# A fused attention and two-MLP kernel: column sums ordered behind the weight conversions, smaller conversion pieces, and a longer lag between the MLP's two products

## The chip, the cores and the metric

The kernel runs on one core of a Trainium2 chip. The metric is the time of one execution on the device in microseconds (us), and the profile is one execution recorded by the hardware. Its engines are PE (TensorE: matmuls; PEld are its weight loads), DVE (VectorE), ACT (ScalarE), POOL (GpSimd) and SP (SyncE, which here issues the DMAs). Each engine works through its own queue in a fixed order.

## The reference, cut to what matters

```python
attn_out = _attn_ref(q, k, v)             # 4 x 8 heads, 576 positions, 64 wide; window of 128, bias by distance
x = attn_out.transpose(0, 2, 1, 3).reshape(2304, 512)
h = x @ moe_w_in                          # 512 x 2048
g = s * np.maximum(h, 0) ** 2 + b
x = g @ moe_w_out                         # 2048 x 512
h = np.maximum(x @ moe2_w_in, 0)
return h * h @ moe2_w_out
```

`s` and `b` are single numbers, so the kernel computes the first MLP without them and applies them to its result: it is scaled by `s`, and `b` times the column sums of `moe_w_out` is added. The weights reach the kernel as 64-bit floats, that is as two 32-bit words each.

## The kernel before, in words

**Blocks.** The 2304 rows of x are worked on in nine blocks of 256: eight blocks (batch 0 to 3, first and second 256 positions) and one "tail" block, with the last 64 positions of every batch. Attention of a block goes by pairs of heads (`pair_unit`): scores on PE (L245), bias and row maximum on DVE (L186), exponentials on ACT (L190), division by the row sum on DVE (L268), transposes on PE (L270), product with v on PE (L281), and a split of the result into two parts (high and low) for the MLP.

**The MLP.** `mlp` runs over 16 steps f for each block: `first` makes a 128-row piece of the hidden layer (twelve matmuls, L357), ACT and DVE square it and split it into high and low (L367, L368, L99, L102), and `last` adds its share to the output (twelve matmuls, L394 in the first MLP; L403 in the second). Between the two lies a lag: `last` of a step is placed after `first` of the step that comes LAG = 2 later, and 1 later in the second MLP, whose blocks are 512 rows wide. The squared and split piece lies in a tile `g` with three buffers (`gw`, two buffers, for the wide blocks). `behind` is a list of pieces of other work (attention units, loads, conversions) that are placed between the steps, spread over the share `span` of them. The last two blocks of the first MLP, block 7 and the tail, run as one `mlp` call, the tail's steps six behind (`lead`); their `behind` holds `sum_column` (the product of the column sums with ones, L544, and its scaling by b) and two `fetch_y` (loads of first-MLP results and half results, and scaling by s and b, for the second MLP).

**The weights.** Each MLP's weights are four groups of four steps (512 of 2048 hidden columns). `group_loads` makes for each group a list of loads and a list of conversions. A load brings a part of w_in or w_out to a staging tile `st` (L151, on SP's queue). `convert` then turns the pairs of words into a 32-bit float and splits it in high and low: ACT on the low word (L119), DVE joins the sign (L120), ACT scales the high word (L121), DVE shifts it (L122), POOL adds the two (L123), ACT copies the high part (L99), and DVE subtracts it (L102). For the first MLP a conversion handles a whole load: parts of 128x1024 (twice the width of one step's piece; 14 of these), and for the last group's w_out four of 128x512. The second MLP has 32 parts of 128x512. The staging tiles of the first three groups are the places of the fourth group's weights, so a load waits until the conversion before it in that place is done. The second MLP's weights take the places of the first one's.

**The column sums.** `sum_rows` (L499 to L502) adds the high and low parts of each of 16 row blocks of w_out to `csum`, 32 additions on POOL. In the program they stand between the steps of blocks 3 to 6.

**The order of work.** The program is written as one sequence, with `zipped` mixing lists in given ratios. A planner then orders each engine's instructions: earlier in the program means a higher priority, but what is ready by its simulated timeline may go ahead of what isn't, as the column sums do. `tc.issue_after(x)` makes the instructions that it encloses come after x on the engine of x.

## Time and profile before

| | us |
|---|---|
| median of three runs | 1007.93 (1007.28 to 1010.74) |
| profiled execution | 1010.16 |
| its span, first to last instruction | 1008.4 |
| PE busy in the span | 974.3 (97%) |
| DVE busy | 522.2 (52%) |
| ACT busy | 490.2 (49%) |
| POOL busy | 130.4 (13%) |
| mean granted PE clock | 0.985 of full speed |

The span is shown below in 40 slices of 25.2 us; each digit is the busy share in tenths (9 is 90% or more), PEclk the granted clock in tenths, and DMA the share of the 16 DMA engines. The first slices hold the attention's first units and the conversion of the first MLP's weights, slices 20 to 27 the conversion of the second MLP's.

```profile
PE   6899889999999999999999899999999999999997
DVE  6997998443564444544265787754223222432222
ACT  7977766454555445554355666664222312322221
POOL 4653655000000000000010312310000000000000
PEclk9799989999999999999999999999999999999999
DMA  8135423111221211211052444422000100100001
```

### The profile page before, as it was taken

To read this page: it belongs to the slowest core of one execution; us is meant where nothing else is said; L and a number is where in the kernel's file an instruction comes from. 1 tells how busy PE (TensorE), PEld (TensorE's weight loads), DVE (VectorE), ACT (ScalarE), POOL (GpSimd) and SP (SyncE) were. 2 spreads that over 40 slices of the span, in tenths; PEclk is the share of its full clock that TensorE was granted. 3 is DMA by queue.
4 is the path that set the end of the run, shared out by engine and by line. 5 is a ranking of instruction groups with operands and counts; after the bars stand their busy time and mean duration, and the time that the engine had idled before them with its cause. 6 is when DMAs were issued, how large, how long until landed. Compare 5 with 4: busy or idle time off the path is not lost.

```text
span 1008.4 us, 16815 instructions
## 1 busy us (share of the span) xinstructions
PE 974.3 (97%) x6504; PEld 854.1 (85%) x6504; DVE 522.2 (52%) x1236; ACT 490.2 (49%) x1157; POOL 130.4 (13%) x118
## 2 busy tenths in 40 slices
PE   6899889999999999999999899999999999999997
PEld 4689778999989999899999888778888888898886
DVE  6997998443564444544265787754223222432222
ACT  7977766454555445554355666664222312322221
POOL 4653655000000000000010312310000000000000
PEclk9799989999999999999999999999999999999999
DMA  8135423111221211211052444422000100100001
GB/s 333 43 129 167 162 88 106 53 53 35 60 67 46 72 34 52 75 54 39 9 184 74 131 173 147 147 83 74 11 1 5 59 1 0 43 1 22 1 1 42
DMA packets 46928, 72.39 MB, mean 72 GB/s; under 512 B 6656, under 2 KB 27136, under 8 KB 46848
## 3 DMA queue, kind: packets, MB, share of 16 engines
q1 hardware_dynamic: 46848, 71.32, 21.8%
q8 instruction: 51, 0.84, 0.3%
q14 instruction: 29, 0.24, 0.1%
HBM read 59.77 MB, written 11.53 MB: 71 GB/s over the span
## 4 chain that ended last, share of the span: by engine, by line
PE 75%; DVE 9%; DMA 9%; ACT 4%; issue 2%; SPq 0%; POOL 0%; ACTq 0%; DVEq 0%; POOLq 0%
PE ob L403 15%; PE hb L357 14%; PE ha L357 13%; PE oa L394 13%; DMA st<-w_in 4%; PE oc L394 3%; PE s L245 3%; PE hc L357 3%; PE u L281 3%; DMA st<-w_out 2%; PE hbtail L357 2%; PE t L270 2%; PE obtail L403 2%; DVE wol L102 1%; DVE wil L102 1%
## 5 line engine op out<-in xcount | busy, mean ns | idle before, releaser
L394 PE MATMUL oa<-ga,woh 128*128 128x256 f32 x960 | 189.6, 289 | 7.3 <-ACT ga L99 3.9
L403 PE MATMUL ob<-woh,gb 128*128 128x512 f32 x512 | 168.9, 391 | 1.4 <-ACT gb L99 1.3
L394 PEld LDWEIGHTS oa<-ga,woh 128*128 128x128 f32 x960 | 152.2, 192 | 14.0 <-DVE ga L102 5.2
L394 PE MATMUL oa<-ga,wol 128*128 128x256 f32 x480 | 135.6, 286 | 0.1
L368 DVE SCALAR_TENSOR_TENSOR rb<-hb,rb 128x512 f32<-128x512 f32 x64 | 44.1, 690 | 147.4 <-ACT rb L367 147.2
L403 PEld LDWEIGHTS ob<-woh,gb 128*128 128x128 f32 x512 | 95.9, 188 | 23.8 <-ACT gb L99 3.3
L367 ACT ACTIVATE rb<-hb 128x512 f32<-128x512 f32 x64 | 38.2, 597 | 156.5 <-PE hb L357 152.0
L123 POOL TENSOR_TENSOR st<-st 128x512 int32<-128x512 int32 (+1 forms) x50 | 70.3, 1407 | 235.1 <-DVE st L122 177.4
L403 PE MATMUL ob<-wol,gb 128*128 128x512 f32 x256 | 99.7, 389 | 0.0
L394 PEld LDWEIGHTS oa<-ga,wol 128*128 128x128 f32 x480 | 92.2, 192 | 1.2 <-issue 0.9
L368 DVE SCALAR_TENSOR_TENSOR ra<-ha,ra 128x256 f32<-128x256 f32 x120 | 50.0, 419 | 62.9 <-ACT ra L367 62.4
L102 DVE TENSOR_TENSOR ga<-ra,ga 128x256 fp32r<-128x256 f32 x120 | 65.8, 552 | 29.0 <-ACT ga L99 28.4
L99 ACT ACTIVATE ga<-ra 128x256 fp32r<-128x256 f32 x120 | 49.5, 416 | 42.4 <-DVE ra L368 41.7
L102 DVE TENSOR_TENSOR gb<-rb,gb 128x512 fp32r<-128x512 f32 x64 | 45.5, 711 | 44.0 <-ACT gb L99 43.8
L367 ACT ACTIVATE ra<-ha 128x256 f32<-128x256 f32 x120 | 45.0, 378 | 43.6 <-PE ha L357 39.0
L99 ACT ACTIVATE gb<-rb 128x512 fp32r<-128x512 f32 x64 | 40.4, 632 | 47.7 <-DVE rb L368 35.6
L120 DVE SCALAR_TENSOR_TENSOR st<-st 128x512 int32<-128x512 int32 (+1 forms) x50 | 47.3, 950 | 26.3 <-ACT st L119 25.8
L119 ACT ACTIVATE st<-st 128x512 int32<-128x512 uint32 (+1 forms) x50 | 40.5, 814 | 35.2 <-DMA st<-w_out 19.3
L403 PEld LDWEIGHTS ob<-wol,gb 128*128 128x128 f32 x256 | 48.1, 188 | 9.7
L190 ACT ACTIVATE pr<-pr,nd 128x256 f32<-128x256 f32 (+1 forms) x96 | 45.1, 473 | 3.8 <-DVE nd L186 3.4
L121 ACT ACTIVATE st<-st 128x512 f32<-128x512 f32 (+1 forms) x50 | 40.5, 813 | 7.0 <-DVE st L120 7.0
L186 DVE CUSTOM_DVE_ANT_0 pr<-s,bases 128x256 f32<-128x256 f32 (+1 forms) x96 | 32.1, 386 | 19.4 <-PE t L270 15.0
(204 smaller groups left out, 2387.1 us busy)
## 6 DMA issues: line engine op xcount, KB each, us to landing
st<-w_out SPq DMA_DIRECT2D x20, 512.0 KB, 3.9
st<-w_in SPq DMA_DIRECT2D x8, 1024.0 KB, 6.8
st<-w_in SPq DMA_DIRECT2D x16, 512.0 KB, 4.8
st<-w_out SPq DMA_DIRECT2D x6, 1024.0 KB, 8.9
raw<-qkv SPq DMA_DIRECT2D x36, 128.0 KB, 2.6
xib<-acc SPq DMA_DIRECT2D x9, 512.0 KB, 4.4
out<-obb SPq DMA_DIRECT2D x16, 256.0 KB, 2.0
raw<-qkv SPq DMA_DIRECT2D x24, 160.0 KB, 2.9
```

Source lines behind the costliest of these rows:

```text
L99: return nc.scalar.activation(o, i, AF.Copy)
L102: nc.vector.tensor_tensor(o, a, b_, ALU.subtract)
L119: nc.scalar.activation(l32, l32.bitcast(U32), AF.Copy, scale=2.0 ** -29)
L120: nc.vector.scalar_tensor_tensor(l32, h32, -2 ** 31, l32, ALU.bitwise_and, ALU.bitwise_or)
L121: nc.scalar.activation(h32.bitcast(F32), h32.bitcast(F32), AF.Copy, scale=2.0 ** -112)
L123: nc.gpsimd.tensor_tensor(l32, h32, l32, ALU.add)
L190: nc.scalar.activation(pr, pr, AF.Exp, bias=nmx, scale=-1.0, accum_out=den)
L357: nc.tensor.matmul(ph, w_[:, cc, j * P:(j + 1) * P], x_[:, cc, :], start=(k == 0), stop=(k == 3 * NCC - 1))
L367: nc.scalar.activation(r, ph, AF.Relu)
L368: nc.vector.scalar_tensor_tensor(r, ph, 0.0, r, ALU.max, ALU.mult)
L394: nc.tensor.matmul(po[o // 2][:, (o % 2) * BLK:(o % 2 + 1) * BLK], w_[:, j, o * P:(o + 1) * P], g[:, gi, :], start=(start and n == 0 and o ...
L403: nc.tensor.matmul(po[t], g[:, gi, t * P:(t + 1) * P], w_[:, j, :], start=(start and n == 0), stop=(stop and n == 2))
```

## The change

Four things change. The 32 additions of the column sums come after the last conversion's addition on POOL (`adds[-1]`; when `sum_rows` runs, all of the first MLP's conversions are in the program, and none of the second's). A load of the first MLP's weights is converted in pieces of 128x512, two for a load of twice that, and the lists that mix conversions with other work take correspondingly more of them at a time. Once the attention is done (`"bp" in pools`) the lag is 4 instead of 2 where the block is 256 wide, and two of every five steps take their `g` from the buffers of `gw`, which makes five tiles. And in the call for the last two blocks of the first MLP, two empty entries stand ahead of `sum_column`, with a span of 0.6 instead of 0.9.

```diff
@@ -104,6 +104,7 @@
 
     n_g = [0]
 
+    adds = []
     marks = []
 
     def convert(words, hi, lo):
@@ -120,7 +121,7 @@
         nc.vector.scalar_tensor_tensor(l32, h32, -2 ** 31, l32, ALU.bitwise_and, ALU.bitwise_or)
         nc.scalar.activation(h32.bitcast(F32), h32.bitcast(F32), AF.Copy, scale=2.0 ** -112)
         nc.vector.tensor_scalar(h32, h32, 3, None, ALU.logical_shift_left)
-        nc.gpsimd.tensor_tensor(l32, h32, l32, ALU.add)
+        adds.append(nc.gpsimd.tensor_tensor(l32, h32, l32, ALU.add).ins)
         split(hi, lo, l32.bitcast(F32), act_copy, dve_sub)
 
     last_load = []
@@ -150,15 +151,18 @@
             with tc.issue_after(last_load[0]) if last_load else nullcontext():
                 wdma.append(nc.sync.dma_start(t, src).ins)
 
-        def conv(i):
+        def conv(i, y):
             _, k, n, step = parts[i]
             if k not in wts[g]:
                 for j in (k, k + 1):
                     wts[g][j] = wp.tile([P, GF, DM], F32R, tag=f"{GTAGS[j]}{g}", name=f"{GTAGS[j]}{g}")
             hi, lo = wts[g][k], wts[g][k + 1]
-            part = (slice(None), slice(n, n + step)) if k else (slice(None), slice(None), slice(n * P, (n + step) * P))
-            convert(places.pop(i).rearrange("p a (n w) -> p a n w", w=2), hi[part], lo[part])
-        return [[lambda f=f, i=i: f(i) for i in range(len(parts))] for f in (load, conv)]
+            at = slice(n + y, n + y + 1) if k else slice((n + y) * P, (n + y + 1) * P)
+            part = (slice(None), at) if k else (slice(None), slice(None), at)
+            words = places[i].rearrange("p a (n w) -> p a n w", w=2)
+            convert(words[:, y:y + 1] if k else words[:, :, y * P:(y + 1) * P], hi[part], lo[part])
+        return [[lambda i=i: load(i) for i in range(len(parts))],
+                [lambda i=i, y=y: conv(i, y) for i, part in enumerate(parts) for y in range(part[3])]]
 
 
     first = {}
@@ -362,7 +366,10 @@
                 gh = pools["bp"].tile([P, 2, w], F32R, tag="gw", name=f"g{nm}_{f}")
                 r = pools["bp"].tile([P, w], F32, tag="rw", name=f"r{nm}_{f}", bufs=1)
             else:
-                gh = mp.tile([P, 2, BLK], F32R, tag="g", name=f"g{nm}_{f}", bufs=3)
+                if "bp" in pools and n_g[0] % 5 > 2:
+                    gh = pools["bp"].tile([P, 2, 2 * BLK], F32R, tag="gw", name=f"g{nm}_{f}")[:, :, :BLK]
+                else:
+                    gh = mp.tile([P, 2, BLK], F32R, tag="g", name=f"g{nm}_{f}", bufs=3)
                 r = mp.tile([P, BLK], F32, tag="r", name=f"r{nm}_{f}")
             nc.scalar.activation(r, ph, AF.Relu)
             nc.vector.scalar_tensor_tensor(r, ph, 0.0, r, ALU.max, ALU.mult)
@@ -381,7 +388,7 @@
                 behind.pop(0)()
             first(f, n)
             done += 1
-            if len(todo) > (1 if w > BLK else LAG):
+            if len(todo) > (1 if w > BLK else 4 if "bp" in pools else LAG):
                 last()
         while todo:
             last()
@@ -479,17 +486,17 @@
     new_x(blocks[0])
     a0 = [lambda hp=hp: first_pair(0, hp) for hp in range(H // 2)]
     run(a0[:2] + l0[:1])
-    run(zipped((a0[2:], 1), (c0, 1), (l0[1:], 1)))
+    run(zipped((a0[2:], 1), (c0, 2), (l0[1:], 1)))
     new_x(blocks[1])
     a1 = [lambda hp=hp: first_pair(1, hp) for hp in range(H // 2)]
     xs = [xt[blocks[0]], xt[blocks[1]]]
-    half(0, zipped((l1, 1), (c1, 1), (a1, 2)))
+    half(0, zipped((l1, 1), (c1, 2), (a1, 2)))
     a2 = attn(2)
     half(1, zipped((a2, 3), (l2, 1)))
     xs.append(xt[blocks[2]])
     a3 = attn(3)
-    half(2, zipped((c2, 2), (a3[:2], 1)))
-    other(0, zipped((l3, 2), (c3, 2), (a3[2:5], 1)), 0.6)
+    half(2, zipped((c2, 4), (a3[:2], 1)))
+    other(0, zipped((l3, 2), (c3, 3), (a3[2:5], 1)), 0.6)
     pending = a3[5:] + attn(4)
     for i in range(1, NHALF):
         other(i, pending[:4])
@@ -498,8 +505,9 @@
     nc.sync.dma_start(b_sb, b_in.partition_broadcast(P))
     def sum_rows(g, j):
 
-        for w in (wts1[g][2], wts1[g][3]):
-            nc.gpsimd.tensor_tensor(csum, csum, w[:, j, :].bitcast(F32), ALU.add)
+        with tc.issue_after(adds[-1]):
+            for w in (wts1[g][2], wts1[g][3]):
+                nc.gpsimd.tensor_tensor(csum, csum, w[:, j, :].bitcast(F32), ALU.add)
 
     nc.gpsimd.memset(csum, 0.0)
     sums = [lambda g=g, j=j: sum_rows(g, j) for g in range(NG) for j in range(GF)]
@@ -556,7 +564,7 @@
     y0 = []
     mlp([(f"a{i}", xt.pop(blocks[i]), finish1(f"a{i}", acc_dram[i])),
          (f"a{LAST}", x_tail, finish1(f"a{LAST}", acc_dram[LAST]))], wts1, second_t, FS,
-        [sum_column] + [lambda u=u: y0.append(fetch_y(u)) for u in range(2)], 0.9, 6)
+        [lambda: None] * 2 + [sum_column] + [lambda u=u: y0.append(fetch_y(u)) for u in range(2)], 0.6, 6)
 
     def in_bp(i, nm):
         return bp.tile([P, 1, 2 * DM], I32, tag="st", name=nm, bufs=3)
```

## Rows read from the trace of the kernel before

**Rows 1.** The page, part 1: busy time, its share, instructions of each engine.

```profile
PE 974.3 (97%) x6504; PEld 854.1 (85%) x6504; DVE 522.2 (52%) x1236; ACT 490.2 (49%) x1157; POOL 130.4 (13%) x118
```

**Rows 2.** Engine time by stretch: us, busy us (instructions), granted clock, DMA share, GB/s.

```profile
10.00:50.00 40.00, 34.57 (x160) 23.57 (x161) 37.81 (x88) 39.02 (x95) 17.61 (x11) 0.82 0.43 162
50.00:110.00 60.00, 59.70 (x503) 53.40 (x503) 52.36 (x115) 43.25 (x99) 27.66 (x17) 0.98 0.47 159
110.00:140.00 30.00, 22.95 (x156) 18.54 (x155) 29.11 (x45) 20.93 (x47) 19.50 (x12) 0.83 0.38 123
140.00:160.00 20.00, 20.00 (x166) 19.52 (x164) 16.00 (x23) 11.79 (x22) 11.55 (x8) 1.00 0.25 81
170.00:210.00 40.00, 40.00 (x352) 37.14 (x350) 18.71 (x64) 20.15 (x54) 0.00 (x0) 1.00 0.12 37
560.00:600.00 40.00, 34.59 (x259) 32.04 (x258) 30.21 (x53) 26.80 (x58) 8.55 (x8) 1.00 0.46 152
680.00:1000.00 320.00, 320.00 (x1502) 268.62 (x1501) 96.98 (x151) 84.38 (x153) 0.00 (x0) 1.00 0.05 17
```

**Rows 3.** Timeline of VectorE, 128 to 136 us: start, us, line, operation, count.

```profile
128.77 4.17 DVE L268 TENSOR_SCALAR pr<-pr,nd 128x256 f32<-128x256 f32 x4
132.86 1.21 DVE L120 SCALAR_TENSOR_TENSOR st<-st 128x1024 int32<-128x1024 int32 x1
134.66 0.67 DVE L120 SCALAR_TENSOR_TENSOR st<-st 128x512 int32<-128x512 int32 x1
```

**Rows 4.** VectorE by line and form, 168 to 210 us: busy us, mean ns of one.

```profile
L102 DVE TENSOR_TENSOR gc<-rc,gc 128x256 fp32r<-128x256 f32 x13 | 6.4, 489 | 4.0 <-ACT gc L99 4.0
L268 DVE TENSOR_SCALAR pr<-pr,nd 128x256 f32<-128x256 f32 x12 | 3.4, 346 | 0.0
```

**Rows 5.** GpSimd by line and form, 110 to 140 us.

```profile
L123 POOL TENSOR_TENSOR st<-st 128x1024 int32<-128x1024 int32 x3 | 7.6, 2538 | 8.9 <-DVE st L122 8.9
L502 POOL TENSOR_TENSOR csum<-csum,woh 128x512 f32<-128x512 f32 x4 | 6.6, 1652 | 3.3 <-ACT woh L99 3.0
L502 POOL TENSOR_TENSOR csum<-csum,wol 128x512 f32<-128x512 f32 x4 | 5.3, 1325 | 0.2
L123 POOL TENSOR_TENSOR st<-st 128x512 int32<-128x512 int32 x1 | 1.0, 1044 | 1.9 <-DVE st L122 1.9
```

**Rows 6.** Timeline of TensorE, 46 to 133 us; in brackets idle time before, and its releaser.

```profile
48.70 0.38 PE L357 MATMUL ha<-x0h,wih 128*128 128x256 f32 x1 [2.41 <-DVE ra L368]
...
130.13 0.41 PE L270 MATMUL t<-ident,pr 128*128 128x128 f32 x2 [1.65 <-DVE pr L268]
131.38 0.69 PE L270 MATMUL t<-ident,pr 128*128 128x128 f32 x2 [0.85 <-DVE pr L268]
132.82 0.47 PE L270 MATMUL t<-ident,pr 128*128 128x128 f32 x1 [0.75 <-ACT pt L99]
```

**Rows 7.** The tile csum: duration ns (least, median, most), first and last start.

```profile
L502 POOL TENSOR_TENSOR csum<-csum,woh x16: 1271/1456/2250, 38.0 to 165.4; 128x512 f32<-128x512 f32 x16
L502 POOL TENSOR_TENSOR csum<-csum,wol x16: 1263/1352/2340, 41.5 to 167.1; 128x512 f32<-128x512 f32 x16
L544 PE MATMUL pc<-ones,csum x8: 250/250/271, 503.7 to 504.5; 128*128 128x1 f32 x8
```

**Rows 8.** The chain that ended last, 488 to 590 us: start, us, what.

```profile
488.56 1.44 PE ha L357 x12
584.46 5.47 DMA xib<-acc
```
**Rows 9.** ScalarE by line and form, whole span.

```profile
L119 ACT ACTIVATE st<-st 128x512 int32<-128x512 uint32 x36 | 24.4, 678 | 32.6 <-DMA st<-w_out 18.2 <-DMA st<-w_in 14.3
L119 ACT ACTIVATE st<-st 128x1024 int32<-128x1024 uint32 x14 | 16.1, 1164 | 2.6 <-DMA st<-w_in 1.4 <-DMA st<-w_out 1.1
```

**Rows 10.** Waits of TensorE, 490 to 680 us: us in total, times, longest.

```profile
PE oa L394 <- ACT ga L99: 3.9, 4, 1.5
PE pc L544 <- ACT xoa L99: 0.7, 1, 0.7
```


## The prediction

> **What bounds the kernel now.** I read the page's busy line first, then a table of engine time by stretch, then the timeline around the places where TensorE isn't full, and last its waits. TensorE is busy 974.3 of 1008.4 us [rows 1], so what can be won is what it loses, and the table says where [rows 2]: from 170 us on it is full (40.00 of 40, later 320.00 of 320) except for one hole, 560 to 600 us, with 34.59 of 40. The front is the other place. In 10 to 50 us ScalarE is full (39.02 of 40) with VectorE close behind (37.81); in 50 to 110 us TensorE is full (59.70 of 60) and sets the pace; in 110 to 140 us VectorE is full (29.11 of 30), TensorE has 22.95 of 30 and a granted clock of 0.83, that is part of the time at 1.2 GHz instead of 2.4. That stretch holds 156 matmuls; at the rate of the next 20 us, which hold 166, they take 18.8 us, so about 11 us are lost in it (an estimate, since the mix of shapes differs). In 560 to 600 us there are 259 matmuls: at the same 8.3 per us 31.2 us of work, or 32.6 with the dozen of double width at its end, so some 7.4 us are lost.
>
> Why VectorE is full around 125 us is seen in the timeline: four L268 operations take 4.17 us at 128.77 us [rows 3], though one takes 346 ns where GpSimd stands still [rows 4]. Beside them GpSimd runs column sums (eight in 110 to 140 us, 6.6 + 5.3 us) [rows 5]. So a VectorE operation that works on SBUF alone waits for the GpSimd operation under way: (4.17 - 4 x 0.346) / 4 = 0.7 us each here. TensorE's transposes wait behind it: 1.65, 0.85 and 0.75 us of idle time [rows 6].
>
> **The change part by part.**
>
> *The column sums go behind the last conversion.* All 32 start between 38.0 and 167.1 us [rows 7]. Ordered behind the last add of a conversion, which here comes shortly before the last sums, they find nothing else on GpSimd and run as one block: 16 x 1.456 + 16 x 1.352 = 44.9 us [rows 7], from about 160 to 205 us. Nobody waits for them: the column product starts at 503.7 us [rows 7], and what stands behind them on GpSimd's queue is the attention's memsets for its last rows and the second MLP's adds, far later.
>
> What leaves the front: of the 11 us lost in 110 to 140 us I give the sums half, 5.5 us, because they are 11.9 us of GpSimd's time there and the conversions' own adds, which stay, nearly all the rest [rows 5]. Of the 2.41 us wait that ends at 48.70 us [rows 6] I give them half, 1.2 us, and 0.3 us for small waits after 160 us. Together 7 us; bounds nothing, if other work refills the holes, and 14 us, if the 11 and the 2.41 go whole.
>
> What comes to 165 to 210 us: in 168 to 210 us VectorE has 13 subtractions for gc and 12 L268 [rows 4], 25 operations that work on SBUF alone, and in 170 to 210 us 18.71 of 40 us of work [rows 2]. At 0.7 us each the block adds 17.5 us: 36 of 40. The MLP's own chain stands this: with the lag of two, four blocks of twelve matmuls of 1.44 us [rows 8], 5.76 us, lie between the end of a first product and its second one, and only relu, square, copy and subtraction are to be done in them. What may not stand it is the attention: a set of four L268 with transposes ordered behind it. Such a burst cost 3.25 us of idle time [rows 6]. Three lie in the stretch (12 L268); I charge one in full and take the others as hidden by products queued ahead: 3.25 us. Bounds: nothing, since TensorE is full there now and the lag may cover all, and 2 x (3.25 + 5.1) = 16.7 us for two in full, where 5.1 us is the whole clock deficit of the worst stretch, 30 x (1 - 0.83) [rows 2].
>
> *Pieces of 128x512.* 14 conversions of 128x1024 become 28. One ScalarE operation costs 2 x 0.678 - 1.164 = 0.19 us more [rows 9]; with three alike 0.58 us a conversion, 8.1 us in all. One VectorE operation costs 2 x 0.67 - 1.21 = 0.13 us more [rows 3]; three make 0.4 us, 5.5 us in all. It counts in 10 to 50 us, with ScalarE full: some five of the 14 lie there, 0.58 x 5 = 2.9 us if nothing hides it. Against it stand an earlier first piece (128 columns can be used before the next 128 are converted) and a shorter lock: the adds of the large pieces took 2538 ns in the mean in 110 to 140 us, that of a small one 1044 [rows 5], though there are twice as many. I take 1 us of loss, between a gain of 3 and a loss of 3. The loads keep number, size and place on SP's queue; a staging buffer is free when its second piece is done, about when the one large piece was.
>
> *A lag of four after the attention.* It touches the last two blocks of the first MLP (about 505 to 610 us) and the tail block of the second. TensorE waits there 3.9 us for ScalarE's copies into ga [rows 10]; the count above says 7.4 us, since a restart costs more than the idle time shown. One cause: ScalarE's queue holds the scaling of the next y ahead of such a copy and stands until its load, 5.47 us from 584.46 us, has landed [rows 8]; conversions hold it in the same way. Two more steps in flight give 2 x 2.88 = 5.76 us more before a second product is due, and the five tiles for g (three old, two of the wider kind) suffice for five in flight. I take 5 us gained: transient waits vanish, while what is a lack of throughput (VectorE has 30.21 us of work [rows 2] for what would be 32.6 us) comes back at the start of the second MLP, whose lag stays one. Bounds 0 and 7.4 us. The places of w_out become free two steps later; hidden, because a group converts its four pieces of w_in first, and worth up to 5.76 us if not. In the tail block TensorE is full now [rows 2], so it gains nothing, and that full queue is the cover; without it a wait for a wide tile would cost one step, 2.9 us.
>
> *The column product later, the y loads closer.* The product goes from step 0 to step 7 of the two blocks; the first y from step 9 to 11, the second from 18 to 15 (five entries over 32 x 0.6 = 19 steps). Before the product TensorE waits 0.7 us [rows 10] for the old banks to be emptied; I take 0.5 us gained, bounds 0 and 0.7. The second y comes three steps earlier, on SP's queue ahead of the same loads as before; no cost, as both are placed before the next y's load starts at 584.46 us [rows 8]; if that cover is gone, such a load, 5.47 us.
>
> **The sum.** -7 + 3.25 + 1 - 5 - 0.5 = -8.25 us. The profiled execution took 1010.16 us, 1.8 us around its span, which gives 1001.9. It stands 2.2 us above the median of the runs shown, 1007.93, which gives 999.7. I forecast 1000.0 us, with a range of its own from 994 (a full hole, hidden bursts) to 1004 (half of both gains).
>
> A rule of the Trainium skill speaks against the first part. "SBUF — State Buffer", section "Who interferes with whom", says that VectorE and GpSimd share a pair of ports as an exclusive lock, for a VectorE operation with two SBUF inputs too, and that whichever comes second waits for the other's whole instruction; the four L268 above bear it out [rows 3]. By that rule moving the sums saves no lock time, it is paid where they go.
>
> **The rivals.**
>
> *The block of sums starves VectorE (slower).* Thrown together, 25 operations that each wait for a whole sum of 1.4 us are 35 us on top of 18.71: 54 us of VectorE work in 40. TensorE, whose order is fixed, pays two bursts in full with the clock, and the sum is -8.25 - 3.25 + 16.7 = +5 us: 1013. It decides from the point where a burst is late by more than the 5.76 us of the lag. For it: VectorE was late like this at 125 us. Against: there it had conversions besides, and the sums in 50 to 110 us left TensorE full [rows 2]. 14%.
>
> *Nothing moves.* ScalarE sets 10 to 50 us and TensorE 50 to 110 us, the 8.1 and 5.5 us of extra work refill 110 to 140 us, and the lag only shifts the lack of throughput into the second MLP: gains of 3 us against costs of 2, 1007. 13%.
>
> *More than that.* The front's holes close and the clock stays up (-14), the halves gain (-3), the bursts hide, the late hole goes whole (-7.4 - 0.7): -25. About 20 of it would be 988. For it: the waits in the front are single and short. Against: ScalarE is full early. 21%.
>
> **How the numbers follow.** Forecast 52%, slower rival 14%, none 13%, more 21%. The range for 8 in 10 is 989 to 1010. A measurement of this kernel can tell about 0.3%, 3 us, from no change. Faster than 1004.9: nearly all of the 52 and the 21, 0.72; within 0.3% 0.13; slower 0.15.
>
> **What would show it.** Sums in one block after the last conversion; L268 near 350 ns before 160 us and near 1 us in the block; TensorE above 26 of 30 us in 110 to 140 us with a clock over 0.9; at most 4 us of idle time in 160 to 210 us; under 2 us of waits for ga after 540 us. The forecast is wrong if the block makes TensorE wait over 8 us, if conversions end later than now, or if the late hole only moves behind 600 us.

## The result and the profile after

The changed kernel takes 1022.1 us (median of four runs, 1020.18 to 1024.34), the kernel before, in runs beside it, 1008.86 (1007.28 to 1010.74): a ratio of 1.013, 95% interval 1.0112 to 1.0148. The forecast was 1000.0 us, faster, with a range of 989 to 1010. It is slower by 13 us. Times given as measured are medians; one execution of act_halves, of 2342.2 us, is left out.

First the page's busy line of the kernel after (part 1, answering [rows 1]), then engine time by stretch, with the columns of [rows 2] and one stretch more, 600 to 680 us.

```profile
PE 981.8 (96%) x6504; PEld 859.4 (84%) x6504; DVE 524.1 (51%) x1278; ACT 493.5 (48%) x1199; POOL 130.1 (13%) x132
```

```profile
10.00:50.00 40.00, 33.81 (x153) 21.79 (x153) 37.24 (x109) 39.63 (x107) 13.92 (x13) 0.83 0.44 160
50.00:110.00 60.00, 59.03 (x486) 53.30 (x487) 41.41 (x116) 43.09 (x110) 9.95 (x8) 0.95 0.46 150
110.00:140.00 30.00, 24.45 (x160) 20.07 (x160) 23.79 (x64) 22.62 (x55) 8.43 (x6) 0.77 0.47 141
140.00:160.00 20.00, 19.61 (x166) 19.10 (x165) 13.39 (x25) 11.41 (x25) 5.18 (x4) 1.00 0.27 80
170.00:210.00 40.00, 35.46 (x268) 31.62 (x267) 28.99 (x49) 15.72 (x43) 37.80 (x29) 0.91 0.15 47
560.00:600.00 40.00, 40.00 (x335) 40.00 (x335) 32.65 (x60) 28.52 (x60) 10.60 (x9) 1.00 0.47 152
600.00:680.00 80.00, 73.49 (x344) 57.74 (x343) 60.41 (x89) 53.08 (x97) 19.97 (x19) 1.00 0.44 138
680.00:1000.00 320.00, 320.00 (x1502) 268.67 (x1501) 97.59 (x152) 85.86 (x155) 0.00 (x0) 1.00 0.05 17
```

The same last stretch but one in the kernel before:

```profile
600.00:680.00 80.00, 78.64 (x367) 64.11 (x366) 55.05 (x88) 53.17 (x94) 20.17 (x18) 1.00 0.40 125
```

Read them against [rows 2] by the matmuls in brackets. The front up to 110 us did not get better: 153 matmuls for 160 in 10 to 50 us, 486 for 503 in 50 to 110. 110 to 140 us has 160 for 156, at a lower clock. 170 to 210 us, full before, has lost 84 of 352 matmuls. The late hole (560 to 600 us) is closed, and 600 to 680 us has 73.49 us where it had 78.64.

To see where time goes, I count TensorE's steps. A step is the twelve matmuls of one first product, in order; the table gives when step 24, 36 and 112 of the first MLP begin, when its last second product begins, and when second-product step 16 of the second MLP begins. All kernels run the same 6504 matmuls. The labels are those of the experiments below. Each row is one execution, the profiled one.

```
us              step 24  step 36  step 112  last of MLP 1  MLP 2, step 16
before            156.5    199.7     504.6          612.2           705.4
after             158.8    213.1     516.6          612.5           717.7
order_only        155.0    207.6     512.5          618.1           710.7
pieces_only       167.5    214.4     519.4          625.7           719.2
lag_only          156.9    200.2     504.2          600.3           705.6
before_nosums     150.8    194.5     496.3          601.8           694.9
after_nosums      157.9    204.6     505.0          601.1           705.0
sums_late         149.9    193.5     494.5          600.6           693.9
late_lag          151.7    195.1     496.0          592.1           697.4
pieces_late       158.5    205.1     505.5          612.0           705.5
paired_late       153.9    200.2     501.1          609.5           703.0
act_halves        156.3    198.9     499.8          606.7           700.5
vec_halves        155.7    199.8     500.7          607.1           700.7
```

After stands 2.3 us behind before at step 24, 13.4 at step 36, 12.0 at step 112; the lag of four brings it level by the end of the first MLP (612.5 and 612.2), and 90 us later all 12 us are lost again.

Differences of a few us in this table are to be read with care. order_only, before_nosums and sums_late run the same instructions in the same order on every engine and DMA queue up to 160 us (the sums apart, which none of them runs there), and yet order_only reaches step 24 four to five us later than the other two. Its first weight load to a staging tile lands at 10.4 us, theirs at 8.8 and 9.2.

**The block of sums.** Tile csum of the kernel after (answers [rows 7]), then VectorE in the block by line (answers [rows 4]; mean ns of one stands second behind the bar), and its timeline there (as [rows 3]):

```profile
L510 POOL TENSOR_TENSOR csum<-csum,woh x16: 1260/1289/1357, 164.8 to 208.2; 128x512 f32<-128x512 f32 x16
L510 POOL TENSOR_TENSOR csum<-csum,wol x16: 1266/1360/1792, 166.1 to 209.6; 128x512 f32<-128x512 f32 x16
```

```profile
L272 DVE TENSOR_SCALAR pr<-pr,nd 128x256 f32<-128x256 f32 x8 | 10.6, 1375 | 0.0
L102 DVE TENSOR_TENSOR gc<-rc,gc 128x256 fp32r<-128x256 f32 x10 | 10.2, 1030 | 1.9 <-ACT gc L99 1.9
L375 DVE SCALAR_TENSOR_TENSOR rc<-hc,rc 128x256 f32<-128x256 f32 x8 | 3.3, 413 | 0.2 <-ACT rc L374 0.2
```

```profile
169.30 5.44 DVE L272 TENSOR_SCALAR pr<-pr,nd 128x256 f32<-128x256 f32 x4
174.66 0.68 DVE L102 TENSOR_TENSOR wol<-st,woh 128x512 fp32r<-128x512 f32 x1
175.26 1.48 DVE L102 TENSOR_TENSOR gc<-rc,gc 128x256 fp32r<-128x256 f32 x1
```

The sums run as one block, as predicted. L272 (L268 of before) takes 1375 ns there, about the length of a sum, where it took 346 without one [rows 4]; the four from 169.30 us hold VectorE for 5.44 us, four times a sum, and the last subtraction of a w_out piece and the next one for gc stand behind them. The square (L375, which reads PSUM) keeps its 413 ns. TensorE's timeline at that place (answers [rows 6]; idle time before, in brackets) shows who pays:

```profile
165.44 0.39 PE L361 MATMUL hc<-x0h,wih 128*128 128x256 f32 x1 [2.19 <-DVE rc L375]
172.11 0.44 PE L274 MATMUL t<-ident,pr 128*128 128x128 f32 x2 [0.15 <-DVE pr L272]
176.79 0.58 PE L401 MATMUL oc<-gc,woh 128*128 128x256 f32 x1 [3.93 <-DVE gc L102]
```

**The late hole.** TensorE's waits, 490 to 680 us, of the kernel after (answers [rows 10]; us in total, times, longest):

```profile
PE ob L410 <- ACT gb L99: 4.0, 8, 1.5
PE ob L410 <- DVE gb L102: 2.0, 5, 0.5
PE ha L361 <- ACT xoa L99: 0.7, 1, 0.7
PE oa L401 <- DVE ga L102: 0.4, 1, 0.4
```

Two lines of the same view of before that [rows 10] does not show:

```profile
PE oa L394 <- DVE ga L102: 1.3, 2, 0.7
PE ob L403 <- ACT gb L99: 1.3, 3, 0.6
```

The waits for ga have fallen from 5.2 us (ScalarE's 3.9 and VectorE's 1.3) to 0.4, and waits for gb, in the second MLP, have grown from 1.3 us to 6.0 in their place.

### The profile page after: what moved, and what is told of

The parts are those of the page before. It is cut to its first block, busy times and chain, and to the rows that moved or that the text cites. A ratio compares the mean times of both kernels' runs of the same rounds, so it can differ in the third digit from the quotient of the medians.

```text
span 1020.6 us, 16912 instructions
## 1 busy us (share of the span) xinstructions
PE 981.8 (96%) x6504; PEld 859.4 (84%) x6504; DVE 524.1 (51%) x1278; ACT 493.5 (48%) x1199; POOL 130.1 (13%) x132
## 4 chain that ended last, share of the span: by engine, by line
PE 77%; DVE 10%; DMA 6%; ACT 4%; issue 2%; POOL 1%; SPq 0%; DVEq 0%; ACTq 0%; POOLq 0%
PE ob L410 15%; PE hb L361 14%; PE ha L361 14%; PE oa L401 14%; PE s L249 3%; PE oc L401 3%; PE hc L361 3%; PE u L285 3%; DMA st<-w_out 3%; PE hbtail L361 2%; PE t L274 2%; PE obtail L410 2%; DMA st<-w_in 2%; DVE st L121 2%; DVE wil L102 1%
## 5 line engine op out<-in xcount | busy, mean ns | idle before, releaser
L375 DVE SCALAR_TENSOR_TENSOR rb<-hb,rb 128x512 f32<-128x512 f32 x64 | 44.2, 690 | 145.7 <-ACT rb L374 145.5
L124 POOL TENSOR_TENSOR st<-st 128x512 int32<-128x512 int32 x64 | 74.0, 1165 | 283.8 <-DVE st L123 220.5
L375 DVE SCALAR_TENSOR_TENSOR ra<-ha,ra 128x256 f32<-128x256 f32 x120 | 50.2, 419 | 67.6 <-ACT ra L374 67.2
L102 DVE TENSOR_TENSOR ga<-ra,ga 128x256 fp32r<-128x256 f32 x120 | 53.4, 449 | 31.8 <-ACT ga L99 31.3
L102 DVE TENSOR_TENSOR gb<-rb,gb 128x512 fp32r<-128x512 f32 x64 | 44.8, 700 | 46.5 <-ACT gb L99 46.3
L121 DVE SCALAR_TENSOR_TENSOR st<-st 128x512 int32<-128x512 int32 x64 | 47.4, 758 | 26.9 <-ACT st L120 26.8
L120 ACT ACTIVATE st<-st 128x512 int32<-128x512 uint32 x64 | 41.6, 678 | 26.6 <-DMA st<-w_in 13.9
L122 ACT ACTIVATE st<-st 128x512 f32<-128x512 f32 x64 | 42.5, 689 | 13.9 <-DVE st L121 13.8
L190 DVE CUSTOM_DVE_ANT_0 pr<-s,bases 128x256 f32<-128x256 f32 (+1 forms) x96 | 31.9, 386 | 29.6 <-PE t L274 14.7
```

Source lines behind the costliest of these rows:

```text
L102: nc.vector.tensor_tensor(o, a, b_, ALU.subtract)
L120: nc.scalar.activation(l32, l32.bitcast(U32), AF.Copy, scale=2.0 ** -29)
L121: nc.vector.scalar_tensor_tensor(l32, h32, -2 ** 31, l32, ALU.bitwise_and, ALU.bitwise_or)
L122: nc.scalar.activation(h32.bitcast(F32), h32.bitcast(F32), AF.Copy, scale=2.0 ** -112)
L124: adds.append(nc.gpsimd.tensor_tensor(l32, h32, l32, ALU.add).ins)
L375: nc.vector.scalar_tensor_tensor(r, ph, 0.0, r, ALU.max, ALU.mult)
```

## The experiments

### One part at a time

**order_only**: only the sums ordered behind the last conversion's add.

```diff
-        nc.gpsimd.tensor_tensor(l32, h32, l32, ALU.add)
+        adds.append(nc.gpsimd.tensor_tensor(l32, h32, l32, ALU.add).ins)
...
+        with tc.issue_after(adds[-1]):
+          for w in (wts1[g][2], wts1[g][3]):
```

> The kernel before with the column sums ordered behind the last conversion's add, and nothing else of the change. Theory A (the block of sums is what costs: VectorE's SBUF operations and the attention's transposes behind them wait in 165 to 205 us): the front to 156 us is up to 5 us earlier than before, the block loses about 11 us, so 1013 to 1018 us, with TensorE under 37 of 40 us busy in 170 to 210 us. Theory B (the sums' move gains in front what it loses later, and the loss of the whole change is that of the smaller pieces): 1004 to 1010 us.

Measured: 1014.38 us, ratio 1.0056 (1.0041 to 1.0071). By the table it is 1.5 us ahead of before at step 24 and 7.9 behind at step 36: the block costs 9.4 us between the two. In 170 to 210 us:

```profile
170.00:210.00 40.00, 35.00 (x277) 31.90 (x276) 32.15 (x54) 15.20 (x43) 36.59 (x27) 0.91 0.11 34
```

It has the signature of the kernel after (35.46 us, clock 0.91) without any pieces, so the loss in this stretch is the block's. The part that was to bring the most makes the kernel slower by itself. Against before_nosums (below), which has no sums at all, order_only is 14.1 us slower; 8.9 of that arise between steps 24 and 36.

**pieces_only**: the changed `conv` and the changed mixing ratios; sums and lag as before.

```diff
-    run(zipped((a0[2:], 1), (c0, 1), (l0[1:], 1)))
+    run(zipped((a0[2:], 1), (c0, 2), (l0[1:], 1)))
...
-    half(2, zipped((c2, 2), (a3[:2], 1)))
+    half(2, zipped((c2, 4), (a3[:2], 1)))
```

> The kernel before with the first MLP's conversions in pieces of 128x512, the sums as before. Theory A: the fixed cost of twice as many operations is nearly hidden, 1008 to 1012 us. Theory B: the pieces eat what the moved sums would have given in the front, 1015 us or more here, where the sums still lie in the front.

Measured: 1023.69 us, ratio 1.0147 (1.0132 to 1.0162). Costed at +1 us, this is the dearest part. It is 11.0 us behind at step 24. Its largest wait of TensorE, 10 to 170 us (1.2 us in before):

```profile
PE ha L360 <- DVE x0l L102: 6.7, 2, 3.8
```

**lag_only**: the lag of four, the two further places for `g`, the later column product.

```diff
-            if len(todo) > (1 if w > BLK else LAG):
+            if len(todo) > (1 if w > BLK else 4 if "bp" in pools else LAG):
```

> The kernel before with the lag of four, the five g tiles and the later column product. Theory A (the conversions of the second MLP's weights, through three staging tiles, set the pace from 545 to 680 us; the lag only moves TensorE's lost time from 560 to 600 us to 600 to 680 us): within 2 us of before, TensorE full in 560 to 600 us and about 8 us short in 600 to 680 us. Theory B (the hole came back only because the change had delayed everything): 1001 to 1004 us, 600 to 680 us no worse than before.

Measured: 1009.69 us, ratio 1.0012 (0.9998 to 1.0026): nothing. The table shows the gain and its return: 11.9 us ahead at the end of the first MLP, 0.2 behind at step 16 of the second. Two stretches of its trace:

```profile
560.00:600.00 40.00, 39.32 (x314) 38.41 (x313) 33.28 (x57) 27.39 (x60) 10.60 (x9) 1.00 0.46 152
600.00:680.00 80.00, 73.63 (x316) 56.92 (x315) 53.25 (x78) 48.53 (x85) 16.63 (x16) 1.00 0.37 119
```

The hole of [rows 2] is filled, and 600 to 680 us gives back 5.0 us of TensorE's time. Part of the 11.9 us is order: ten fewer matmuls stand ahead of that last product than in before (4705 for 4715).

### What the sums cost, before and after

**before_nosums** and **after_nosums** are the two kernels without the 32 additions of the column sums; the term with b is left out of their result.

```diff
-    sums = [lambda g=g, j=j: sum_rows(g, j) for g in range(NG) for j in range(GF)]
+    sums = [lambda g=g, j=j: sum_rows(g, j) for g in range(NG) for j in range(GF)][:0]
```

> The kernel before with the 32 additions of the column sums left out (csum stays zero, so the term with b is left out of the result). Theory A (in the front the sums delay VectorE, but most of that is off TensorE's path): 1004 to 1009 us, and the smaller pieces with the lag and without sums (1009.1 us) then stand at 0 to 5 us of cost. Theory B (the front pays for the sums nearly in full, and the pieces eat it): 1000 us or less, so that pieces cost 9 us or more even without any sums.

> The kernel after with the 32 additions of the column sums left out (csum stays zero, so the term with b is left out of the result). Theory A: the loss in 160 to 210 us goes and the rest stays, about 11 us faster than the kernel after, 1009 to 1013 us. Theory B (VectorE is late there for the conversions, not for the sums): 1018 us or more.

Measured: before_nosums 1000.24 us, ratio 0.9922 (0.9905 to 0.9939); after_nosums 1009.1, ratio 1.0003 (0.9993 to 1.0012). So the sums cost 8 us in the front of before, 13 us as a block in the kernel after, and everything else that the change does costs 8.9 us with no sum in sight. 13 - 8.2 + 8.9 is 13.7 us, near the 13.2 by which after is slower (each kernel was measured beside its own runs of before). Of the 13 us of the block, 7.6 arise between steps 24 and 36 and some 3 more by step 112; no run here shows where those 3 are lost.

### Sums where little else uses VectorE

**sums_late**: the sums wait for the attention's last memset on GpSimd, and the column product comes nine steps into the last two blocks.

```diff
-        nc.gpsimd.memset(pr[:, :Z], 0.0)
+        sets[:] = [nc.gpsimd.memset(pr[:, :Z], 0.0).ins]
...
+        with tc.issue_after(sets[0]):
+          for w in (wts1[g][2], wts1[g][3]):
...
-        [sum_column] + [lambda u=u: y0.append(fetch_y(u)) for u in range(2)], 0.9, 6)
+        [lambda: None] * 3 + [sum_column] + [lambda u=u: y0.append(fetch_y(u)) for u in range(2)], 0.6, 6)
```

> The kernel before with the column sums ordered behind GpSimd's last memset for the attention, so that they run in a block from about 480 us on, and the column product moved to step 9 of the last two blocks. Theory A (a block of sums costs time only where attention stands beside it; the MLP's chain alone is covered by the lag): the time of the kernel without sums within 3 us, TensorE full in 480 to 540 us. Theory B (a block of sums costs 8 to 11 us anywhere): 1013 us or more.

Measured: **999.46 us**, ratio 0.9907 (0.9889 to 0.9926), faster than both kernels and level with leaving the sums out. Tile csum, the stretch beside it, and VectorE's subtraction for ga in 450 to 496 us:

```profile
L504 POOL TENSOR_TENSOR csum<-csum,woh x16: 1277/1290/1357, 451.0 to 493.1; 128x512 f32<-128x512 f32 x16
```

```profile
450.00:496.00 46.00, 45.25 (x394) 43.60 (x393) 21.85 (x45) 16.43 (x46) 42.58 (x34) 1.00 0.10 28
```

```profile
L102 DVE TENSOR_TENSOR ga<-ra,ga 128x256 fp32r<-128x256 f32 x13 | 12.1, 933 | 5.6 <-ACT ga L99 5.6
```

VectorE waits for the sums here too (933 ns for a subtraction that takes 426 in the same stretch of before_nosums), but TensorE loses nothing by it: it has 45.25 of 46 us at full clock, exactly as in before_nosums, which has no sums. Beside the MLP's own chain only four operations of the tail's attention stand there, and the lag of two covers the chain. In 170 to 210 us the same block stood beside eight L272 with transposes ordered behind them. That this is the reason is argued from the two timelines; that the place decides is measured.

### Why the pieces cost eight

**pieces_late**: sums_late with the pieces as in the change. **paired_late**: the same, with the two pieces of a load always in one entry, so that the mixing ratios are those of before.

```diff
+                [lambda i=i, n=part[3]: [conv(i, y) for y in range(n)] for i, part in enumerate(parts)]]
```

> The kernel with the sums after the attention (999.5 us), and the first MLP's conversions in pieces of 128x512 mixed into the other work as in the change. Theory A (the pieces cost by themselves, without any sums beside them): 1006 to 1011 us, the front to the 24th first product 5 to 8 us later. Theory B (the two kernels without sums differ by other things, the lag above all): 999 to 1002 us.

> The same with the two pieces of a load in one entry, so that loads, conversions and attention units are mixed in the ratios of before. Theory A1 (the cost is that of twice as many operations on ScalarE and VectorE, 8.1 and 5.5 us): the same as with pieces mixed singly, within 2 us. Theory A2 (it is the order in which the planner lays single pieces among the attention's operations): within 3 us of 999.5 us.

Measured: pieces_late 1007.99 us, ratio 1.0001 (0.9986 to 1.0017); paired_late 1007.73, ratio 0.9983 (0.9968 to 0.9998). With no sum in the front the pieces still cost 8.5 us, and nearly as much (0.76% for 0.94%) when the mixing ratios are those of before. So it is mainly the operations themselves and not how they are mixed; the mixing may have a share, since paired_late stands 6.6 us behind sums_late at step 112 and pieces_late 11.0. With sums in the front (pieces_only) they cost 14.7.

**act_halves** and **vec_halves** are sums_late with some of the seven operations of a large conversion made twice on halves, the others whole: ScalarE's three, or VectorE's three and GpSimd's add.

```diff
+        for w, _, _ in for_act:
+            with tc.issue_after(marks[-4]) if len(marks) > 3 else nullcontext():
+                nc.scalar.activation(w[..., 0], w[..., 0].bitcast(U32), AF.Copy, scale=2.0 ** -29)
+        for w, _, _ in for_dve:
+            nc.vector.scalar_tensor_tensor(w[..., 0], w[..., 1], -2 ** 31, w[..., 0], ALU.bitwise_and, ALU.bitwise_or)
...
```

> sums_late, with only the three ScalarE operations of every first-MLP conversion of 128x1024 made twice on 128x512; VectorE and GpSimd keep whole tiles. If the fixed time of a ScalarE operation (0.19 us each, 3 more for each of 14 converted tiles: 8.1 us on an engine that is full from 10 to 50 us) is what makes the pieces cost 8.5 us: 1005 to 1008 us. If it is VectorE's and GpSimd's operations: 999 to 1001 us.

> sums_late, with only the VectorE and GpSimd operations of every first-MLP conversion of 128x1024 made twice on 128x512; ScalarE keeps whole tiles. If ScalarE's fixed time is the cost of the pieces: 999 to 1001 us. If the pieces cost by VectorE's and GpSimd's fixed times and by the two engines' lock-step (more, shorter operations that wait for each other): 1004 to 1008 us. If both ScalarE's and these are half of it: each kernel 1003 to 1004.

Measured: act_halves 1005.15 us, ratio 0.9958 (0.9943 to 0.9973); vec_halves 1005.2, ratio 0.9975 (0.9959 to 0.9991). Neither engine group is the cause alone: each adds more than half, 0.51% and 0.68% on sums_late's 0.9907, and both together (pieces_late) 0.94%, which the intervals do not tell from the sum of the two. At step 112 they stand 5.3 and 6.2 us behind sums_late, pieces_late 11.0. The busy lines (page, part 1) of sums_late, act_halves, vec_halves and pieces_late:

```profile
PE 967.4 (97%) x6504; PEld 852.3 (85%) x6504; DVE 508.0 (51%) x1236; ACT 490.2 (49%) x1157; POOL 123.0 (12%) x118
```

```profile
PE 970.1 (97%) x6504; PEld 854.0 (85%) x6504; DVE 507.6 (51%) x1236; ACT 494.3 (49%) x1199; POOL 124.3 (12%) x118
```

```profile
PE 969.7 (97%) x6504; PEld 853.3 (85%) x6504; DVE 507.2 (51%) x1278; ACT 490.0 (49%) x1157; POOL 128.6 (13%) x132
```

```profile
PE 975.2 (97%) x6504; PEld 857.3 (85%) x6504; DVE 508.7 (50%) x1278; ACT 494.3 (49%) x1199; POOL 128.8 (13%) x132
```

42 more operations cost ScalarE 4.1 us, 0.1 us each, and act_halves 5.7 us of time. In vec_halves 14 more adds cost GpSimd 5.6 us, 0.4 us each. VectorE's busy line does not move, but its conversions do: L121, L123 and L102 of sums_late's conversions add up to 126.0 us, the same three operations of vec_halves to 131.7, 0.14 us for each of 42 more. What hides it is that other operations of VectorE became shorter, such as these two (sums_late, then vec_halves; whole span):

```profile
L194 DVE TENSOR_SCALAR nd<-nd 128x4 f32<-128x4 f32 x32 | 9.8, 308 | 21.6 <-ACT pr L191 19.5 <-ACT f_0wih L191 1.2 <-ACT f_2woh L191 0.8
L102 DVE TENSOR_TENSOR ga<-ra,ga 128x256 fp32r<-128x256 f32 x120 | 63.8, 534 | 26.6 <-ACT ga L99 25.8
```

```profile
L211 DVE TENSOR_SCALAR nd<-nd 128x4 f32<-128x4 f32 x32 | 6.6, 205 | 22.5 <-ACT pr L208 21.0 <-ACT f_0wih L208 1.4
L102 DVE TENSOR_TENSOR ga<-ra,ga 128x256 fp32r<-128x256 f32 x120 | 60.6, 510 | 25.5 <-ACT ga L99 24.5 <-PE oa L412 0.5
```

So the pieces add busy time on all three engines, some 4, 5 and 6 us, and 8.5 us of it reaches the total. A conversion is one chain through the three engines, so what one of its links loses can hold up the next. That the chain is why is an inference; that each group alone costs more than half is measured. VectorE's share and GpSimd's were not taken apart.

### Why the lag gives nothing

**late_lag_st3** and **late_lag_st4**: sums_late with the lag of four, the sums' tile and the tile xj moved into buffers shared with the results, which open after the attention, and three or four staging tiles for the second MLP's conversions.

```diff
-    csum = const.tile([P, DM], F32, tag="csum", name="csum")
...
+    csum = bp.tile([P, DM], F32, tag="raw", name="csum")
...
-        return bp.tile([P, 1, 2 * DM], I32, tag="st", name=nm, bufs=3)
+        return bp.tile([P, 1, 2 * DM], I32, tag="st", name=nm, bufs=4)
```

> As the run with the sums after the attention, with the lag of four and the five g tiles as well, and with csum and the small load tile in buffers shared with the results (to make room as the next run needs it). Theory A (the conversions' staging tiles set the pace to 680 us): within 2 us of the run with the sums after the attention alone, with 600 to 680 us short by 5 us or more of TensorE time. Theory B: 3 us or more faster.

> As the run before it, with four staging tiles instead of three for the second MLP's weights. Theory A (load, conversion and release of three staging tiles are the loop that sets the pace): at least 3 us faster than with three, TensorE above 76 of 80 us in 600 to 680 us and the last conversion 5 us or more earlier. Theory B (ScalarE and VectorE have no more throughput, whatever the tiles): within 1 us of it.

Measured: 1032.98 us, ratio 1.0235 (1.0214 to 1.0257), and 1035.56, ratio 1.0279 (1.0245 to 1.0312). These miss their question. The tile opens only when the attention is done, so the sums started at 496 us instead of 451, and the column product, in TensorE's order, held everything (late_lag_st3):

```profile
550.07 1.87 PE L546 MATMUL pc<-ones,csum 128*128 128x1 f32 x8 [26.87 <-POOL csum L506]
```

What follows is only that this product must not come before its sums.

**nosums_lag_st3** and **nosums_lag_st4** ask it without the sums: before without the sums, with the lag of four and three or four staging tiles. The column product multiplies a constant tile, so the term with b in the result is not the right one, and the tile xj shares the results' buffers to make room.

> The kernel before without the sums, with the lag of four, and with the small load tile in the results' buffers; the column product multiplies the identity in place of csum, so the b term of the result is wrong and its time is kept. Control of the next run. Theory A (three staging tiles set the pace to 680 us): within 2 us of the kernel before without the sums (1000.2 us), TensorE 5 us or more short in 600 to 680 us. Theory B: 3 us or more faster.

> The control with four staging tiles for the second MLP's weights. Theory A (the loop of load, conversion and release): 3 us or more faster than the control, the last conversion at least 5 us earlier. Theory B (ScalarE and VectorE have no more throughput): within 1.5 us of it.

Measured: 998.13 us, ratio 0.9894 (0.9876 to 0.9912), and 1000.9, ratio 0.9926 (0.9902 to 0.9949), where before_nosums has 0.9922 (0.9905 to 0.9939). With three tiles the lag is 2.1 us ahead of before_nosums, which the overlapping intervals do not settle, and TensorE is 2.9 us short in 600 to 680 us: neither theory's signs. The fourth tile gives no speed: it is 2.8 us slower than three. By stretch, nosums_lag_st3 and then nosums_lag_st4:

```profile
560.00:600.00 40.00, 37.82 (x272) 35.27 (x271) 31.82 (x54) 26.47 (x55) 10.86 (x9) 1.00 0.52 170
600.00:640.00 40.00, 38.02 (x161) 29.36 (x160) 33.94 (x50) 29.46 (x50) 12.22 (x10) 1.00 0.46 147
640.00:680.00 40.00, 39.07 (x172) 31.97 (x172) 17.71 (x27) 17.45 (x31) 3.12 (x3) 1.00 0.12 40
```

```profile
560.00:600.00 40.00, 35.73 (x268) 33.68 (x267) 36.33 (x58) 28.70 (x58) 12.43 (x11) 1.00 0.58 191
600.00:640.00 40.00, 36.99 (x158) 29.02 (x157) 32.86 (x51) 31.93 (x59) 14.51 (x10) 1.00 0.50 158
640.00:680.00 40.00, 40.00 (x179) 33.11 (x178) 10.38 (x15) 9.24 (x15) 0.00 (x0) 1.00 0.00 1
```

With the fourth tile the conversions do end sooner (their last add starts at 635.4 us instead of 648.8, and GpSimd has nothing left after 640 us), so three tiles did hold them up. But TensorE then loses earlier instead of later, 7.3 us of the 120 where three tiles lose 5.1. What falls is the theory that this loop sets the kernel's time.

**late_lag**: sums_late and the lag of four with its two further places for `g`, nothing else.

> The kernel before with the column sums behind the attention (as in sums_late) and the lag of four with its two extra places for squares; the sums stay in a tile of their own, so they run at 451-494 us as in sums_late, not behind a tile that opens only after the attention. Theory (the second MLP's conversions are bound by ScalarE's and VectorE's work between 560 and 680 us, and the lag only moves TensorE's loss within that stretch): 997 to 1001 us, no different from sums_late's 999.5; TensorE busy in 560-680 us 113 to 115 us of 120, as in all versions so far. Rival (with no sums and no late column product in the way the lag is worth the 5 us of the prediction): 993 to 995 us, TensorE busy 118 us or more of 120.

Measured: 1001.26 us, ratio 0.9926 (0.9912 to 0.994), no faster than sums_late. By stretch, sums_late and then late_lag:

```profile
560.00:600.00 40.00, 35.90 (x254) 33.04 (x253) 33.63 (x58) 27.36 (x58) 9.40 (x8) 1.00 0.43 144
600.00:640.00 40.00, 39.72 (x183) 32.43 (x182) 28.30 (x45) 26.94 (x47) 10.82 (x10) 1.00 0.50 158
```

```profile
560.00:600.00 40.00, 39.19 (x286) 36.73 (x285) 33.32 (x56) 26.90 (x57) 8.84 (x9) 1.00 0.46 152
600.00:640.00 40.00, 35.22 (x147) 26.73 (x146) 30.16 (x42) 25.38 (x44) 10.92 (x11) 1.00 0.48 146
```

3.3 us won in the first stretch, 4.5 lost in the second; in the table it is 8.5 us ahead at the end of the first MLP and 3.5 behind at step 16 of the second, of which 1.5 stood at step 112 already. TensorE is busy 112.8 of 120 us in 560 to 680 us, close to the 113 to 115 of the theory. The rival, that the lag is worth its 5 us once sums and product are out of the way, falls.

## Why the prediction was wrong, point by point

**"The column sums go behind the last conversion", the -7.** The size was right for a front without sums: before_nosums gains 8 us, and 5.7 of them by step 24. L272 did fall to 347 ns before 160 us (its row, 80 to 160 us):

```profile
L272 DVE TENSOR_SCALAR pr<-pr,nd 128x256 f32<-128x256 f32 x12 | 3.6, 347 | 0.0
```

But the front's gain did not reach the total, since the pieces took it in the same stretch (after_nosums reaches step 24 7.1 us later than before_nosums): TensorE has 24.45 of 30 us in 110 to 140 us at a clock of 0.77, where the prediction wanted over 26 and 0.9.

**"I charge one in full", the +3.25 for the block.** This step failed. Order_only shows 9.4 us between steps 24 and 36, and on top of the pieces the block costs 7.6 there (54.3 us between the two steps in after, 46.7 in after_nosums). VectorE did not even get as full as I had worked out (28.99 us in 170 to 210 us, not 36): not its total counts but the order in its queue. One burst of four took 5.44 us, where the one that I priced had 4.17, and with the last subtraction of a conversion behind it the subtraction for gc came so late that TensorE waited 3.93 us; the clock, 0.91 over 40 us, cost 3.6 us of full speed. My own rows held both prices: one burst in full is 3.25 us of idle time, and with the clock deficit of 5.1 it is 8.35, close to what was measured. I charged the first alone, and put the clock into the upper bound and the rival. (Of the 3.25 us, 0.75 stand in [rows 6] as a wait for ScalarE's copy, not for an L268.)

The rule that I set against this part, the Trainium skill's "SBUF — State Buffer", section "Who interferes with whom" (the lock is held for a whole instruction), agrees with the trace: the block's L272 last 1375 ns, as long as a sum. I named it and kept the sum as it was.

**"Pieces of 128x512", the +1.** This step failed most: 8.5 to 8.9 us without sums beside them (pieces_late, after_nosums). I had worked out 0.58 us of ScalarE and 0.4 us of VectorE for each conversion and then counted five of the fourteen, on the ground that ScalarE is full only until 50 us, and set a gain of 3 us against it. More than five count: against sums_late, pieces_late is 1.1 us behind at step 4, 8.6 at step 24 and 11.6 at step 36, so the loss grows as long as conversions run. That the first MLP's steps follow its conversions group by group would explain it, but that is argued. My price for one operation was near the mark for VectorE (0.13 us, measured 0.14) and high for ScalarE (0.19, measured 0.1). The gain from an earlier first piece is not seen (step 4 begins at 61.8 us in pieces_late, 60.7 in sums_late). GpSimd's add, which I credited with a shorter lock, has the largest further time of the seven operations (0.4 us) and was not in the sum.

A sentence of the Trainium skill's "VectorE: DVE Perf Modes", section "The TRN2 errata — SBUF-src ops pay a fixed extra latency per instruction", bears on it: one large tile pays the fixed latency once, many small tiles pay it per tile. The traces agree in kind: 0.1 us of busy time for each further ScalarE operation and 0.14 for each of VectorE. GpSimd's 0.4 us, the largest, is these traces' alone.

**"A lag of four after the attention", the -5.** This step failed. Measured: nothing clear of the noise (lag_only 1.0012, late_lag against sums_late +1.8 us, nosums_lag_st3 against before_nosums -2.1 us). The waits for ga did go, from 5.2 us (I had counted ScalarE's 3.9 alone) to 0.4. "Transient waits vanish" was the wrong half of my own sentence: it is the other case, the lack that "comes back at the start of the second MLP". TensorE's loss in 560 to 680 us stays at 5 to 7 us of 120 in before, sums_late, late_lag, nosums_lag_st3 and nosums_lag_st4, whichever end it falls on. No engine is full there (VectorE 85, ScalarE 80 of 120 us in before), and neither the lag nor a staging tile takes it away; that conversions and copies stand in one order on ScalarE and VectorE fits all of these, but no run here took that order apart. That stays open.

**The column product later, the -0.5.** The 0.7 us wait is still there; it now ends at the first product of the two blocks, which stands where the column product stood. Too small to matter.

**The rivals.** The slower one was right in its sign and in its mechanism, and carries about half of the result; that its 1013 us lies near order_only's 1014.38 is luck, since it holds gains of 7 and 5 us that order_only does not have. It lacked the other half, the pieces. "Nothing moves" was right about the lag and right that extra work refills 110 to 140 us. Of the three things that I wrote would make the forecast wrong, the late hole did only move behind 600 us. Conversions do end later: the last add on GpSimd starts at 163.8 us in the first MLP and 675.9 in the second, in before at 161.0 and 668.3. The block's waits alone stayed under 8 us (TensorE is idle for 6.7 us in 160 to 210 us, 2.2 in after_nosums); the further 4.5 us and the lower clock, 0.90 for 0.97 over these 50 us, come to about 8.

## What to carry to other kernels

Work that makes another engine wait goes where few operations of that engine run and a queue of products covers them, not to the first place where its engine is free: against leaving them out, the same 45 us of sums cost 8 us among the conversions, 13 to 14 beside the attention and nothing at the attention's end. Cutting an operation in two costs a further fixed time on every engine of the chain, and where consumers wait for the chain, much of it arrives: here 8.5 us. An engine's total can hide it, as VectorE's did; look at the lines. A hole that a longer lag fills is won only if the stage behind it has room; look at that stage's own losses first.

## What the hardware showed that I had not expected

- Beside adds that run back to back, L272s in a row get through at one for each add: 1375 ns for an L272 of 347 ns, with adds of 1289 to 1360 ns, while the square, which reads PSUM, keeps 413 ns. Subtractions for gc, mixed with it, take 1030 ns in the mean instead of 489.
- Making one GpSimd add into two of half the size costs 0.4 to 0.5 us (81.0 us for 86 instructions without pieces, 88.1 for 100 with them, in before_nosums and after_nosums), four to five times what it costs on ScalarE and three to four times what it costs on VectorE (0.14 us).
- The same removal of the sums from the front gave TensorE 1.5 us by step 24 in order_only, but 5.7 in before_nosums and 6.6 in sums_late, with the same instructions in the same order up to there. Their granted clock in 110 to 140 us was 0.77, 0.83 and 0.89. The weight loads of order_only landed 1.2 to 1.6 us later from the first staging tile on; why, and why that grew, no run here tells.
